# Chunk-local scores with a carried state, and the transfers that put K~ in chunk order, in a gated linear attention kernel with an MLP

## The chip, the cores and the metric

The kernel runs on one core of one Trainium2 chip. The metric is the device time of one execution in microseconds (us). Most executions of one kernel agree within about 1%; where I give a time it is the median of the runs, with the lowest and the highest where that matters. A single run of the kernel before, 1021.7 us at a granted clock of 0.766 beside six at 837 to 840 us, was slow and is left out. (The granted clock is the share of its full clock that TensorE was given.)

## The reference, cut to what matters

```
# attention: B=4, H=8, S=768, D=48, float32
mag = sqrt(a_re^2 + a_im^2);  a = (a_re + i a_im) * min(mag, 0.999) / (mag + 1e-6)
for t in range(S):
    S_t = a[t] (per row d, complex) * S_{t-1} + k[t] v[t]^T      # D x D, complex
    y[t] = Re( q[t] S_t )
# then an MLP on 3072 rows of 384
x = y as (B*S, H*D)
out = relu(x @ w_in)^2 @ w_out          # 384 -> 2048 -> 384
```

The kernel doesn't step through time. With P(t) the running product of the decays, Q~ = q P and K~ = k / P (rows of 2 x 48 = 96 for real and imaginary parts), and y[t] is the sum over s <= t of (Q~[t] . K~[s]) v[s]. That sum can be cut: scores within a chunk of 128 steps, and everything older through a 96 x 48 state, the sum of K~[s] v[s]^T over the earlier chunks.

## The kernel before

(Excerpts of code, here and below, are shortened; `...` marks cuts.)

A *unit* is 384 steps of one batch entry: the first or the second ("late") half of a sequence. There are 8 units of 4 head pairs. VectorE computes decays, running products and K~, Q~ of one unit; TensorE does the pair work of another and the MLP (`hidden`, `project`) of a third, so three units are in flight.

The inputs lie with three steps in a row: step s = 3p + c is at partition p, place c. That makes the loads long and serves the scan. Scores and output need chunk order instead: step s of chunk j at partition s - 128j. For Q~ and K~ this happens on the way through the transposes (`turn`), whose copies to SBUF interleave the three places. The state product contracts over time, so any order will do if K~ and V have the same: the kernel loads V a second time in row order (`vn`) for it.

```
LOADS: step s = 3p + c at partition p        # C = 128 partitions, W = 3, R = 96, HH = 4
def score(u, i, h):                          # per head: 384 + 128 (+ 256 for two heads at once)
    nc.tensor.matmul(sa[:, 0:3], lhsT=kt[:, 0:C], rhs=qt)          # chunk 0 against all 384
    nc.tensor.matmul(sa[:, 3], lhsT=kt[:, 2*C:3*C], rhs=qt[:, 2*C:3*C])
    dve.tensor_tensor(out=A[:, h, 0:4:3], in0=sa[:, 0:4:3], in1=mask2, op=ALU.mult)
    act.copy(out=A[:, h, 1:3], in_=sa[:, 1:3])                     # unmasked blocks
    ...                                                            # chunk 1 against 256
def keep(u, i):                              # first half only: state at its end
    ... nc.tensor.matmul(ps[:, h], lhsT=K~[:, hh, c], rhs=u["vn"][:, hh, c],
                         start=(c == 0), stop=(c == W - 1))
def mix(u, i):                               # output of a head pair, transposed
    ...
    act.copy(out=yt[0:64 + D], in_=ypair[0:64 + D])
    # to the rows of xT where the MLP wants them: pieces of 48, 32 or 16 rows
    nc.sync.dma_start(out=u["xT"][r % C:r % C + n, r // C], in_=yt[p:p + n])
def hidden(u, f):                            # waits for all of the unit's xT
    ... nc.tensor.matmul(ps, lhsT=w1[:, f, m], rhs=u["xT"][:, m])
```

The loads of the attention inputs, the xT transfers and the stores of the result are issued from SyncE's queue, in order (SPq in the views below); the loads of the weights are on GpSimd's.

Of the kernel before, what the change touches and what calls it, by code (L numbers as in the profile page):

```python
# [9 lines left out]
F32 = mybir.dt.float32  # L10
# [5 lines left out]
ALU = mybir.AluOpType  # L16
# [465 lines left out]
def fast_path(ctx, tc, q, k, v, a_re, a_im, moe_w_in, moe_w_out, out, flag):  # L482
# [54 lines left out]
    mask2 = mask.unsqueeze(1).to_broadcast([C, 2, C])  # L537
# [28 lines left out]
    def convert(i):  # L566
# [20 lines left out]
        if i >= NF:  # L587
            after(first, mark["second"])
        elif i >= EARLY:
            after(first, mark["scanned"])  # L590
# [5 lines left out]
    EARLY = 4  # L596
# [18 lines left out]
    def load(u):  # L615
# [21 lines left out]
        if u["half"] < NHALF - 1:  # L637
            u["vn"] = nat.tile([C, H, W, D], F32, name="vn", tag="vn")
            nc.sync.dma_start(out=u["vn"].rearrange("p h c d -> p h (c d)"),
                              in_=src(v).rearrange(LOADS, c=W))  # L640
# [128 lines left out]
    def product(u, dst, x, y):  # L769
# [16 lines left out]
        return dve.tensor_tensor(out=dst[:, 1], in0=f[0][:, 1], in1=f[1][:, 0], op=ALU.add)  # L786

    def scan(u):
# [16 lines left out]
        for m in range(NM):  # L805
            done = product(u, v4[:, :, m, 1:32], v4[:, :, m, 1:32],
                           inc[:, :, m, 0:31].unsqueeze(3).to_broadcast([C, 2, 31, 4]))
        mark.setdefault("scanned", done)
# [14 lines left out]
    def apply(u, z):  # L823
# [15 lines left out]
        t = pr.tile([C, 2, HH, W, 2, D], F32, name="QK", tag="QK")  # L839
        u.setdefault("QK", {})[z] = t  # L840
        for j in range(2):
            for r in range(2):
                done = dve.tensor_tensor(out=t[:, j, :, :, r], in0=qk[:, j], in1=a[:, r],  # L843
                                         op=ALU.mult)
        if u["n"] == 1:
            mark["second"] = done


    def turn(u, i, c):
# [3 lines left out]
        src = u["QK"][2 * i // HH]  # L853
        ps = trp.tile([R, 4, C], F32, name="tq", tag="tr")
        for j in range(2):
            for h in range(2):
                nc.tensor.transpose(  # L857
                    ps[:, 2 * j + h],
                    src[:, j, (2 * i + h) % HH, c].rearrange("p r d -> p (r d)"), ident)
        act.copy(out=u["T"][i].rearrange("r z (p c) -> r c z p", c=W)[:, c], in_=ps)  # L860

    def score(u, i, h):

        T = u["T"][i]
        if h == 0:
            u.setdefault("A", {})[i] = pr.tile([C, 2, 6, C], F32, name="A", tag="A")
        A = u["A"][i]
        if h < 2:
            qt, kt = T[:, h], T[:, 2 + h]
            sa = scp.tile([C, 4, C], F32, name="sa", tag="sc")  # L870
            nc.tensor.matmul(sa[:, 0:3].rearrange("p n t -> p (n t)"), lhsT=kt[:, 0:C],  # L871
                             rhs=qt, start=True, stop=True)
            nc.tensor.matmul(sa[:, 3], lhsT=kt[:, 2 * C:3 * C], rhs=qt[:, 2 * C:3 * C],  # L873
                             start=True, stop=True)
            dve.tensor_tensor(out=A[:, h, 0:4:3], in0=sa[:, 0:4:3], in1=mask2, op=ALU.mult)  # L875
            act.copy(out=A[:, h, 1:3], in_=sa[:, 1:3])  # L876
            return
        sb = scp.tile([C, 2, 2, C], F32, name="sb", tag="sc")
        for h in range(2):
            qt, kt = T[:, h], T[:, 2 + h]  # L880
            nc.tensor.matmul(sb[:, h].rearrange("p n t -> p (n t)"), lhsT=kt[:, C:2 * C],  # L881
                             rhs=qt[:, C:3 * C], start=True, stop=True)
        dve.tensor_tensor(out=A[:, :, 4], in0=sb[:, :, 0], in1=mask2, op=ALU.mult)  # L883
        act.copy(out=A[:, :, 5], in_=sb[:, :, 1])  # L884
# [3 lines left out]
    def keep(u, i):  # L888

        if u["half"] == NHALF - 1:  # L890
            return
        if i == 0:
            state[u["b"]] = wk.tile([R, H, D], F32, name="S", tag="S", bufs=2)
        ps = trp.tile([R, 2, D], F32, name="kv", tag="tr")
        for h in range(2):
            for c in range(W):
# [197 lines left out]
```

## Time and profile before

| | before |
|---|---|
| median of 3 runs | 840.0 us (837.4 to 845.8) |
| span of the profiled run | 839.8 us |
| TensorE busy / idle / after its last instruction | 748.4 / 83.6 / 7.8 us |
| granted TensorE clock, mean | 0.983 |
| first hidden product of units 0, 2, 3, 7 at | 91.9, 309.3, 402.0, 769.7 us |

Busy, idle and tail add up to the span. The last row gives a clock for the stages: from unit 3 to unit 7 a unit takes (769.7 - 402.0) / 4 = 91.9 us.

The prediction below shows the views. In them PE is TensorE, PEld its loading of weights, DVE VectorE, ACT ScalarE, POOL GpSimd, and SPq the transfers issued from SyncE's queue; L945 is a line of the kernel, and `h<-xT,w` names the tile written and those read.

### The profile page before, as it was taken

The page shows a single profiled execution, that of the slowest core. Times are in us where ns is not written, and L with a number is a line of the kernel's source. Part 1 is how long each engine was busy: PE and PEld are TensorE (multiplying, and loading weights), DVE is VectorE, ACT ScalarE, POOL GpSimd, SP SyncE. Part 2 cuts the span into 40 slices and gives each one's busy share as a digit, 9 for nine tenths or more (in the row PEclk, how much of TensorE's full clock was granted, in tenths as well). Part 3 has the DMA queues.
Part 4 walks back from the last instruction along what each step waited for, and adds up shares of the span by engine and source line. Part 5 has one row for each costly group of instructions (what it writes and reads, how often), then busy time and mean ns, then how long its engine had stood idle before and what let it go on. Part 6 is the DMA issues. An engine that isn't in the chain of part 4 may idle for free.

```text
span 839.8 us, 9088 instructions
## 1 busy us (share of the span) xinstructions
PE 748.4 (89%) x3090; PEld 453.8 (54%) x3090; DVE 507.8 (60%) x1284; ACT 436.2 (52%) x865; POOL 43.6 (5%) x75
## 2 busy tenths in 40 slices
PE   0129995999899889999999999999999989999996
PEld 0016553555566556666566656666666646555553
DVE  5997888889989666078642868097825866300000
ACT  5616883765597159611894259623982235422510
POOL 4101000200000000000000000000000143000000
PEclk9999998999999999999999999999999999999998
DMA  9625301740120150002400150004200278200000
GB/s 284 178 64 166 78 0 29 242 127 26 36 87 8 45 162 6 7 17 55 119 8 8 51 161 1 11 14 124 50 9 17 81 232 269 67 16 27 0 10 23
DMA packets 76920, 61.24 MB, mean 73 GB/s; under 512 B 28736, under 2 KB 71744, under 8 KB 76864
## 3 DMA queue, kind: packets, MB, share of 16 engines
q1 hardware_dynamic: 70720, 35.40, 15.2%
q0 software_dynamic: 6144, 25.17, 9.1%
q8 instruction: 26, 0.43, 0.2%
q14 instruction: 30, 0.25, 0.1%
HBM read 51.12 MB, written 4.72 MB: 66 GB/s over the span
## 4 chain that ended last, share of the span: by engine, by line
PE 59%; DVE 15%; issue 12%; DMA 7%; ACT 4%; SPq 1%; POOL 0%; POOLq 0%; ACTq 0%
PE h L945 21%; PE o L959 19%; PE ypair L914 4%; PE sa L871 4%; PE tq L857 3%; DVE fa L782 3%; PE sb L881 2%; DMA look<-in_moe_w_out_dram 2%; PE kv L898 2%; DMA look<-in_moe_w_in_dram 2%; DVE fb L834 1%; DVE QK L843 1%; PE sa L873 1%; PE ypair L910 1%; ACT QKT L860 1%
## 5 line engine op out<-in xcount | busy, mean ns | idle before, releaser
L945 PE MATMUL h<-xT,w 128*128 128x384 f32 x768 | 274.5, 497 | 10.5 <-DMA xT<-yt 8.5
L959 PE MATMUL o<-w,g 128*128 128x384 f32 x768 | 263.3, 490 | 0.0
L945 PEld LDWEIGHTS h<-xT,w 128*128 128x128 f32 x768 | 140.3, 194 | 89.7 <-DMA xT<-yt 10.5
L959 PEld LDWEIGHTS o<-w,g 128*128 128x128 f32 x768 | 141.3, 191 | 85.9 <-issue 4.1
L860 ACT COPY QKT<-tq 96x512 f32<-96x512 f32 x96 | 80.2, 851 | 48.5 <-PE tq L857 46.4
L950 ACT ACTIVATE g<-h 128x384 f32<-128x384 f32 x128 | 61.9, 488 | 66.6 <-PE h L945 66.2
L857 PE MATMUL tq<-ident,QK 128*96 128x128 f32 x384 | 62.7, 291 | 14.3 <-DVE QK L843 12.7
L857 PEld LDWEIGHTS tq<-ident,QK 128*96 128x96 f32 x384 | 46.5, 134 | 43.7 <-issue 27.5
L951 ACT ACTIVATE g<-g 128x384 f32<-128x384 f32 x128 | 66.4, 523 | 2.4
L875 DVE TENSOR_TENSOR A<-sa,mask 128x256 f32<-128x256 f32 x64 | 26.4, 419 | 58.1 <-PE sa L873 57.9
L782 DVE TENSOR_TENSOR fa<-e 128x192 f32<-128x192 f32 (+1 forms) x56 | 23.8, 455 | 60.0 <-ACT e L755 59.4
L871 PE MATMUL sa<-QKT 96*128 96x384 f32 x128 | 55.3, 514 | 0.1
L914 PE MATMUL ypair<-A,v 128*48 128x256 f32 (+2 forms) x384 | 50.3, 387 | 1.1 <-ACT A L884 1.0
L876 ACT COPY A<-sa 128x256 f32<-128x256 f32 x64 | 23.3, 370 | 52.1 <-DVE A L875 52.1
L843 DVE TENSOR_TENSOR QK<-qk,a 128x576 f32<-128x576 f32 x64 | 44.4, 748 | 0.0
L753 PE MATMUL tot<-ident,last 128*128 128x128 f32 x72 | 14.1, 298 | 31.5 <-ACT last L715 28.7
L1037 DVE TENSOR_SCALAR flag<-cnt 1x1 int32<-1x1 f32 x1 | 0.1, 147 | 69.1 <-PE cnt L1036 69.1
L914 PEld LDWEIGHTS ypair<-A,v 128*48 128x48 f32 x384 | 22.7, 123 | 33.3 <-issue 23.8
L963 ACT COPY ot<-o 128x384 f32<-128x384 f32 x24 | 11.4, 475 | 56.2 <-PE o L959 56.2
L607 POOL DMA_DIRECT2D look<-in_moe_w_in_dram x16 | 12.3, 770 | 510.0 <-DVE A L875 496.0
L884 ACT COPY A<-sb 128x256 f32<-128x256 f32 x32 | 11.8, 368 | 46.6 <-DVE A L883 46.6
L873 PEld LDWEIGHTS sa<-QKT 96*128 96x128 f32 x128 | 24.8, 195 | 17.7 <-issue 2.2
(104 smaller groups left out, 921.0 us busy)
## 6 DMA issues: line engine op xcount, KB each, us to landing
raw<-in_moe_w_in_dram POOLq DMA_DIRECT2D x16, 384.0 KB, 5.1
raw<-in_moe_w_out_dram POOLq DMA_DIRECT2D x16, 384.0 KB, 5.2
look<-in_moe_w_in_dram POOLq DMA_DIRECT2D x16, 384.0 KB, 4.2
look<-in_moe_w_out_dram POOLq DMA_DIRECT2D x16, 384.0 KB, 4.1
a<-in_a_re_dram SPq DMA_DIRECT2D x16, 288.0 KB, 3.0
a<-in_a_im_dram SPq DMA_DIRECT2D x16, 288.0 KB, 3.7
qk<-in_q_dram SPq DMA_DIRECT2D x16, 288.0 KB, 5.0
qk<-in_k_dram SPq DMA_DIRECT2D x16, 288.0 KB, 5.1
```

The costliest lines, as they stand in the source:

```text
L782: dve.tensor_tensor(out=t, in0=x, in1=y[:, j].unsqueeze(1).to_broadcast(shape), op=ALU.mult)
L843: done = dve.tensor_tensor(out=t[:, j, :, :, r], in0=qk[:, j], in1=a[:, r], op=ALU.mult)
L857: nc.tensor.transpose(ps[:, 2 * j + h], src[:, j, (2 * i + h) % HH, c].rearrange("p r d -> p (r d)"), ident)
L860: act.copy(out=u["T"][i].rearrange("r z (p c) -> r c z p", c=W)[:, c], in_=ps)
L871: nc.tensor.matmul(sa[:, 0:3].rearrange("p n t -> p (n t)"), lhsT=kt[:, 0:C], rhs=qt, start=True, stop=True)
L873: nc.tensor.matmul(sa[:, 3], lhsT=kt[:, 2 * C:3 * C], rhs=qt[:, 2 * C:3 * C], start=True, stop=True)
L875: dve.tensor_tensor(out=A[:, h, 0:4:3], in0=sa[:, 0:4:3], in1=mask2, op=ALU.mult)
L914: nc.tensor.matmul(ypair[64 * h:64 * h + D, j * C:L], lhsT=u["v"][:, j, 2 * i + h], rhs=A[:, h, lo:hi].rearrange("p n t -> p (n t)"), star ...
L945: nc.tensor.matmul(ps, lhsT=w1[:, f, m], rhs=u["xT"][:, m], start=(m == 0), stop=(m == NM - 1))
L950: act.activation(out=t, in_=ps, func=AF.Relu)
L951: act.activation(out=t, in_=t, func=AF.Square)
L959: nc.tensor.matmul(u["o"], lhsT=u["g"][f][:, ts(c, C)], rhs=w2[:, f], start=(f == 0), stop=(f == NF - 1))
```

## The change

The intent: TensorE is the bound from about 310 us on, and chunk-local scores need fewer columns. Scores are computed in the three diagonal 128 x 128 blocks only; the past comes in by a state per chunk, built from one product per chunk and head and added up on VectorE. Those products need K~ and V of *one chunk* on the partitions, so row order will not do any more: K~ is put in chunk order by transfers within SBUF, and the second load of V goes. In addition all conversions of weights are kept behind the last Q~, K~ product of the first (or second) unit.

```
@@ apply: K~ in chunk order
+        kc = u["KC", z] = nat.tile([C, NM, HH, R], F32, name="KC", tag=f"KC{z}")
+        for j in range(NM - u["half"]):          # chunks: 3, in a late half 2
+            for c in range(W):                   # the three places of a row
+                lo = -(-(j * C - c) // W)
+                hi = -(-((j + 1) * C - c) // W)
+                first = W * lo + c - j * C
+                nc.sync.dma_start(out=kc[first:first + W * (hi - lo - 1) + 1:W, j],
+                                  in_=out_k[lo:hi, c])
@@ score
+        for j in range(NM):
+            nc.tensor.matmul(sa[:, j], lhsT=T[:, 2 + h, ts(j, C)], rhs=T[:, h, ts(j, C)], ...)
+        dve.tensor_tensor(out=u["A"][i][:, h], in0=sa, in1=mask3, op=ALU.mult)
@@ keep
+        for j in range(n):
+            for h in range(2):
+                nc.tensor.matmul(ps[:, j, h], lhsT=u["KC", hh // HH][:, j, hh % HH],
+                                 rhs=u["v"][:, j, hh], start=True, stop=True)
+        ... # first chunk of a sequence: act.copy, then dve.tensor_tensor(add) onto the state
@@ mix: per chunk, A[j] with v[j], and (if there is a past) the state with Q~ of the chunk
@@ load
-            u["vn"] = ...                        # second load of V
@@ convert
-        if i >= NF: after(first, mark["second"])
-        elif i >= EARLY: after(first, mark["scanned"])
+        after(first, mark["QK", i // NF])
```

128 steps at three a row are 42 or 43 rows: for each chunk and half of the heads there are three transfers, of 43, 43 and 42 rows of 1.5 KB, to every third partition. In all there are 120: 18 in a first-half unit and 12 in a late one.

More of the change, by code (lines that the diff above doesn't have):

```diff
@@ L536, in fast_path @@
                        fill=0.0, base=0, channel_multiplier=-1)
-    mask2 = mask.unsqueeze(1).to_broadcast([C, 2, C])
+    mask3 = mask.unsqueeze(1).to_broadcast([C, NM, C])
     sums = const.tile([C, NU, 7], F32, name="sums")
@@ L586, in convert @@
                                   op0=ALU.bitwise_and, op1=ALU.logical_shift_left)
-        if i >= NF:
-            after(first, mark["second"])
-        elif i >= EARLY:
-            after(first, mark["scanned"])
+        after(first, mark["QK", i // NF])
         dve.scalar_tensor_tensor(out=bits, in0=hi, scalar=0xC0000000, in1=bits,
@@ L594, in convert @@
         dve.tensor_tensor(out=bits, in0=bits, in1=more, op=ALU.add)
-    EARLY = 4
     SPARE = ("fa0", "fa1", "fb0", "fb1")
@@ L636, in load @@
                               in_=src(v).rearrange("h (j s) d -> s j h d", s=C)[:, j])
-        if u["half"] < NHALF - 1:
-            u["vn"] = nat.tile([C, H, W, D], F32, name="vn", tag="vn")
-            nc.sync.dma_start(out=u["vn"].rearrange("p h c d -> p h (c d)"),
-                              in_=src(v).rearrange(LOADS, c=W))
     def flat(t):
@@ L785, in product @@
         dve.tensor_tensor(out=dst[:, 0], in0=f[0][:, 0], in1=f[1][:, 1], op=ALU.subtract)
-        return dve.tensor_tensor(out=dst[:, 1], in0=f[0][:, 1], in1=f[1][:, 0], op=ALU.add)
+        dve.tensor_tensor(out=dst[:, 1], in0=f[0][:, 1], in1=f[1][:, 0], op=ALU.add)
     def scan(u):
@@ L805, in scan @@
         for m in range(NM):
-            done = product(u, v4[:, :, m, 1:32], v4[:, :, m, 1:32],
-                           inc[:, :, m, 0:31].unsqueeze(3).to_broadcast([C, 2, 31, 4]))
-        mark.setdefault("scanned", done)
+            product(u, v4[:, :, m, 1:32], v4[:, :, m, 1:32],
+                    inc[:, :, m, 0:31].unsqueeze(3).to_broadcast([C, 2, 31, 4]))
         if u["half"] < NHALF - 1:
@@ L838, in apply @@
                           op=ALU.add)
-        t = pr.tile([C, 2, HH, W, 2, D], F32, name="QK", tag="QK")
-        u.setdefault("QK", {})[z] = t
-        for j in range(2):
-            for r in range(2):
-                done = dve.tensor_tensor(out=t[:, j, :, :, r], in0=qk[:, j], in1=a[:, r],
-                                         op=ALU.mult)
-        if u["n"] == 1:
-            mark["second"] = done
+        t = pr.tile([C, 2 * HH * W * R], F32, name="QK", tag="QK")
+        half = HH * W * R
+        out_q = u["Q", z] = t[:, 0:half].rearrange("p (h c e) -> p h c e", h=HH, c=W)
+        out_k = t[:, half:2 * half].rearrange("p (c h e) -> p c h e", h=HH, c=W)
+        u["K", z] = out_k
+        for j, o in ((1, out_k.rearrange("p c h e -> p h c e")), (0, out_q)):
+            for r in range(2):
+                done = dve.tensor_tensor(out=o[:, :, :, r * D:(r + 1) * D], in0=qk[:, j],
+                                         in1=a[:, r], op=ALU.mult)
+        mark["QK", u["n"]] = done
+        kc = u["KC", z] = nat.tile([C, NM, HH, R], F32, name="KC", tag=f"KC{z}")
[6 more added lines that the diff above has]
+                                  in_=out_k[lo:hi, c])
     def turn(u, i, c):
@@ L852, in turn @@
             u.setdefault("T", {})[i] = pr.tile([R, 4, L], F32, name="QKT", tag="QKT")
-        src = u["QK"][2 * i // HH]
+        z = 2 * i // HH
         ps = trp.tile([R, 4, C], F32, name="tq", tag="tr")
@@ L856, in turn @@
             for h in range(2):
-                nc.tensor.transpose(
-                    ps[:, 2 * j + h],
-                    src[:, j, (2 * i + h) % HH, c].rearrange("p r d -> p (r d)"), ident)
+                hh = (2 * i + h) % HH
+                src = u["K", z][:, c, hh] if j else u["Q", z][:, hh, c]
+                nc.tensor.transpose(ps[:, 2 * j + h], src, ident)
         act.copy(out=u["T"][i].rearrange("r z (p c) -> r c z p", c=W)[:, c], in_=ps)
@@ L865, in score @@
         if h == 0:
-            u.setdefault("A", {})[i] = pr.tile([C, 2, 6, C], F32, name="A", tag="A")
-        A = u["A"][i]
-        if h < 2:
-            qt, kt = T[:, h], T[:, 2 + h]
-            sa = scp.tile([C, 4, C], F32, name="sa", tag="sc")
-            nc.tensor.matmul(sa[:, 0:3].rearrange("p n t -> p (n t)"), lhsT=kt[:, 0:C],
-                             rhs=qt, start=True, stop=True)
-            nc.tensor.matmul(sa[:, 3], lhsT=kt[:, 2 * C:3 * C], rhs=qt[:, 2 * C:3 * C],
-                             start=True, stop=True)
-            dve.tensor_tensor(out=A[:, h, 0:4:3], in0=sa[:, 0:4:3], in1=mask2, op=ALU.mult)
-            act.copy(out=A[:, h, 1:3], in_=sa[:, 1:3])
-            return
@@ L878, in score @@
-        sb = scp.tile([C, 2, 2, C], F32, name="sb", tag="sc")
-        for h in range(2):
-            qt, kt = T[:, h], T[:, 2 + h]
-            nc.tensor.matmul(sb[:, h].rearrange("p n t -> p (n t)"), lhsT=kt[:, C:2 * C],
-                             rhs=qt[:, C:3 * C], start=True, stop=True)
-        dve.tensor_tensor(out=A[:, :, 4], in0=sb[:, :, 0], in1=mask2, op=ALU.mult)
-        act.copy(out=A[:, :, 5], in_=sb[:, :, 1])
+            u.setdefault("A", {})[i] = pr.tile([C, 2, NM, C], F32, name="A", tag="A")
@@ L886, in fast_path @@
+        sa = scp.tile([C, NM, C], F32, name="sa", tag="sc")
+        for j in range(NM):
+            nc.tensor.matmul(sa[:, j], lhsT=T[:, 2 + h, ts(j, C)], rhs=T[:, h, ts(j, C)],
+                             start=True, stop=True)
+        dve.tensor_tensor(out=u["A"][i][:, h], in0=sa, in1=mask3, op=ALU.mult)
     state = {}
     def keep(u, i):
-        if u["half"] == NHALF - 1:
-            return
-        if i == 0:
+        late = u["half"] > 0
+        n = NM - u["half"]
+        if i == 0 and not late:
@@ L893, in keep @@
             state[u["b"]] = wk.tile([R, H, D], F32, name="S", tag="S", bufs=2)
-        ps = trp.tile([R, 2, D], F32, name="kv", tag="tr")
-        for h in range(2):
-            for c in range(W):
+        total_s = state[u["b"]][:, 2 * i:2 * i + 2]
+        ps = trp.tile([R, NM, 2, D], F32, name="kv", tag="tr")
+        for j in range(n):
+            for h in range(2):
                 hh = 2 * i + h
-                nc.tensor.matmul(
-                    ps[:, h],
-                    lhsT=u["QK"][2 * i // HH][:, 1, hh % HH, c].rearrange("p r d -> p (r d)"),
-                    rhs=u["vn"][:, hh, c], start=(c == 0), stop=(c == W - 1))
@@ L902, in keep @@
-        act.copy(out=state[u["b"]][:, 2 * i:2 * i + 2], in_=ps)
+                nc.tensor.matmul(ps[:, j, h], lhsT=u["KC", hh // HH][:, j, hh % HH],
+                                 rhs=u["v"][:, j, hh], start=True, stop=True)
+        st = pr.tile([R, 2, 2, D], F32, name="St", tag="St")
+        u.setdefault("S", {})[i] = [total_s if late else None, st[:, 0], st[:, 1]]
+        outs = [st[:, 0], st[:, 1], total_s]
+        before = total_s if late else None
+        for j in range(n):
+            if before is None:
+                act.copy(out=outs[j], in_=ps[:, j])
+            else:
+                dve.tensor_tensor(out=outs[j], in0=ps[:, j], in1=before, op=ALU.add)
+            before = outs[j]
@@ L904, in mix @@
     def mix(u, i):
         T, A = u["T"][i], u["A"][i]
-        late = u["half"] > 0
-        if late:
+        for j in range(NM):
+            S_j = u["S"][i][j]
             for h in range(2):
-                nc.tensor.matmul(ypair[64 * h:64 * h + D], lhsT=state[u["b"]][:, 2 * i + h],
-                                 rhs=T[:, h], start=True, stop=False)
-        for j, lo, hi in ((0, 0, 3), (1, 4, 6), (2, 3, 4)):
+                nc.tensor.matmul(ypair[64 * h:64 * h + D, ts(j, C)],
+                                 lhsT=u["v"][:, j, 2 * i + h], rhs=A[:, h, j],
+                                 start=True, stop=S_j is None)
@@ L913, in mix @@
             for h in range(2):
-                nc.tensor.matmul(ypair[64 * h:64 * h + D, j * C:L],
-                                 lhsT=u["v"][:, j, 2 * i + h],
-                                 rhs=A[:, h, lo:hi].rearrange("p n t -> p (n t)"),
-                                 start=(j == 0 and not late), stop=(j == 2))
+                if S_j is not None:
+                    nc.tensor.matmul(ypair[64 * h:64 * h + D, ts(j, C)], lhsT=S_j[:, h],
+                                     rhs=T[:, h, ts(j, C)], start=False, stop=True)
@@ L936, in pair_work @@
                 w.append([lambda i=i: mix(u, i - 1)])
-            w += [[lambda i=i, h=h: score(u, i, h)] for h in range(3)]
+            w += [[lambda i=i, h=h: score(u, i, h)] for h in range(2)]
         w += [[], [lambda: mix(u, NP - 1)]]
```

## The prediction

> **What bounds the kernel now.** I read the page's busy shares and slices first, to see which engine is full and when.
>
> ```profile
> PE 748.4 (89%) x3090; PEld 453.8 (54%) x3090; DVE 507.8 (60%) x1284; ACT 436.2 (52%) x865; POOL 43.6 (5%) x75
> ...
> PE   0129995999899889999999999999999989999996
> ...
> DVE  5997888889989666078642868097825866300000
> ```
>
> A slice is 21 us. TensorE is full from slice 15 (about 310 us) to the end; before that VectorE is as full as TensorE or fuller. So there are two regimes. The windows (busy us of PE, its weight loads, DVE, ACT, POOL) put numbers to them.
>
> ```profile
> 40.00:60.00 20.00, 3.42 (x12) 2.05 (x13) 18.60 (x69) 2.81 (x6) 2.14 (x3) 1.00 0.27 86
> ...
> 240.00:280.00 40.00, 37.66 (x174) 24.03 (x171) 36.39 (x106) 29.76 (x64) 0.00 (x0) 0.98 0.08 23
> ...
> 320.00:360.00 40.00, 40.00 (x169) 24.30 (x168) 10.99 (x23) 29.84 (x59) 0.00 (x0) 1.00 0.02 5
> ```
>
> From 0 to about 300 us, three chains of normalisation, scan and products run on VectorE (first unit's products end at 67.8, second's at 150.4, fourth's at 297). From 310 on TensorE alone is the bound. Busy time overlaps there, so I take what an instruction costs from the distance between starts in the timeline of PE (start, length, ..., count).
>
> ```profile
> 653.66 0.60 PE L857 MATMUL tq<-ident,QK 128*96 128x128 f32 x4
> 654.09 1.14 PE L898 MATMUL kv<-vn,QK 128*96 128x48 f32 x12
> 655.07 0.88 PE L959 MATMUL o<-w,g 128*128 128x384 f32 x2
> ...
> 658.14 1.50 PE L914 MATMUL ypair<-A,v 128*48 128x384 f32 x12
> 659.58 0.55 PE L819 MATMUL bk<-ident,e 128*128 128x128 f32 x3
> 659.96 2.75 PE L959 MATMUL o<-w,g 128*128 128x384 f32 x8
> 662.54 0.81 PE L871 MATMUL sa<-QKT 96*128 96x384 f32 x2
> 663.19 0.38 PE L873 MATMUL sa<-QKT 96*128 96x128 f32 x2
> 663.41 1.78 PE L959 MATMUL o<-w,g 128*128 128x384 f32 x5
> ```
>
> One matmul of the source is two records. Two of 384 columns take 0.65 us (662.54 to 663.19), two of 128 take 0.22, so 0.108 us per 128-column record; twelve kv records 0.98 (654.09 to 655.07, 0.082 each); twelve ypair records 1.44 (658.14 to 659.58).
>
> At the changes of unit the chain of waits shows what TensorE lacks for 2 to 3 us: xT, the transfer of the last head pair.
>
> ```profile
> 299.70 0.50 SPq L624 DMA_DIRECT2D qk<-in_q_dram  x1
> ...
> 302.45 1.60 SPq L624 DMA_DIRECT2D qk<-in_k_dram  x1
> ...
> 310.01 1.15 SPq L927 DMA_DIRECT2D xT<-yt  x2
> ```
>
> In this timeline of the transfer queue, xT stands behind eight input loads that waited for VectorE's products; each issue takes about 0.5 us.
>
> [...]384 columns take 0.65 us, 1.68 ns per column[...]; transposes (one record) take half. [...]ypair streams 2 heads x 768 columns, 2.6 us at 1.68 ns, in 1.44. [...]For 256 elements [...]the trace has 419 for the mask. [...]the trace has 1.9 us to landing for the 24 KB and the 48 KB transfers of xT alike.
>
> **The change, part by part.** There are 32 head pairs (8 units of 4), 16 in a first half of a sequence and 16 in a second ("late") half.
>
> Scores. Before, per head 384+128+256 columns, 0.65+0.22+0.43 = 1.30 us, 2.60 a pair. After, six products of 128 columns, 12 records x 0.109 = 1.31. **-1.3 us per pair** on TensorE.
>
> Output. Before 1.44, plus 0.7 late for the state (the L910 row: 13.6 us busy in 64 records that overlap in twos; four start-to-start take 0.68 to 0.78). After, 128-column records, two heads at once: 0.054 each, 20 of them in a first half, 24 late, plus 0.15 for the ends: 1.23 and 1.45. **-0.2 and -0.7**.
>
> State. First half: six products as before, 12 records, 0. Late: none before, four now, 8 x 0.085 = **+0.7**.
>
> Net on TensorE: -1.5 per first-half pair, -1.3 per late pair, -45 us in all. Only part lies where TensorE is the bound: the pairs of units 3 to 7 run after 310 us, 12 late and 8 first: 12 x 1.3 + 8 x 1.5 = **-27.6 us**. Units 0 to 2 carry 17 us, in the regime shared with VectorE.
>
> ScalarE loses the copies of unmasked scores, 64 x 0.370 + 32 x 0.368 = -35 us; the state copies stay at 16 x 0.237. Off the path after 310; a small help before it.
>
> VectorE: masks were 26.4 + 13.4 = 39.8 us, become 64 of 384 elements, [...]The 64 additions of 96 elements are new, [...]VectorE is 40% idle after 310, so nothing there[...]. The products into QK (64 of 748 ns) keep their size and only change their strides.
>
> Transfers: vn goes (4 of 576 KB). 18 transfers for K~ per first-half unit, 12 per late one, 120 in all, of 43 rows x 1.5 KB, at about 0.5 us of issue: 9 or 6 us of the queue per unit, some 2 us to landing. K~ is computed before Q~, so they start about 1.4 us earlier than the products end. I looked at the order of the transfer queue in both: from unit 3 on, the K~ transfers now stand before the last xT and the big input loads after it. That exchanges eight loads (2.3 MB) for 12 to 18 small ones ahead of xT, and ScalarE's copy to yt no longer stands behind an instruction that waits for those loads. I give **-3 us** over the boundaries, which show idle TensorE of 2.2, 1.7, 1.7 and 3.4 us now.
>
> Conversion. Before 67.8 us VectorE does five conversions' worth (four whole, one in pieces), 0.27+0.47+0.47 = 1.21 us each from starts: 6 us, some of it in gaps. The first unit's products come about 5 us earlier, but all 16 conversions (19.4 us) now fall into the first unit's pair work, which took 25.5 us with 11 of them and 7.7 us of idle VectorE. [...]So only 3 us of the 5 survive. Second and third units: TensorE -5 and -6 us, [...]both near full; I give -4 together. **-7 us before 310.**
>
> Sum: -27.6 - 3 - 7 = -38 us: 840 - 38 = **802 us**. The tail from 770 (hidden and projection of the last unit, 62 us) does not change.
>
> **The rivals.** (a) K~ transfers hold the queue. VectorE's last K~ product of a unit is followed by 6 to 9 issues, 3 to 4.5 us, and only then xT; if yt is ready before them, TensorE waits up to 4 us more at each of 6 boundaries: +24, about 826. For it: 0.5 us per issue. Against it: the eight loads it replaces cost the same issue time and more bytes. (b) The additions tie the PSUM buffer of kv to VectorE's in-order stream; transposes share those two buffers and would wait behind chain instructions. Then part of the 27.6 comes back as idle TensorE: about 815. For it: VectorE's chain now and then stands idle waiting for ScalarE. Against it: the mask already couples them so, and score buffers now come free without a second copy. (c) The first 310 us gain nothing, as VectorE gets more work: about 809. (d) TensorE's bubbles shrink too: from 160 us on, start-to-start times exceed the nominal by some 39 us, with half-clock stretches after idle gaps; fewer stalls could give 10 us more: 792.
>
> **Range and chances.** 802 as the sum; (b) and (c) together lead to about 818, (d) to 790. Range 788 to 818. Faster by over 2% is below 823: that is 17 us, under two thirds of the 27.6 alone, so (b) or (c) would still be faster; (a) in full would miss it. Faster 0.92, within 2% 0.07, slower 0.01.
>
> **What would show it.** Score records: 384 of 128 columns with a start-to-start of 0.11 us; the ypair group of a pair 1.2 to 1.5 us; kv 320 records. Phase lengths after 310: about 88 us per unit for 93. ACT's busy time about 400, DVE's about 520. First unit's products end near 62.5 and its conversions near 90. If (a): PE waits of several us on xT with K~ issues before them in the queue. If (b): PE waits on VectorE's additions before transposes. If the ypair records take 0.1 us each, the heads no longer overlap and the output costs 1 us more per pair. The prediction fails most likely through the ordering of the engines' streams, which the sums do not see.

The sum came to -38 us, that is 802. My estimates of what a mask and an addition would cost VectorE: the 520 us of VectorE and the 90 us at which conversions would end rested on them, and of the -7 us before 310 the -3 of the first unit; the other -4 are my estimate for the second and third units.

## More of the kernel before

One group of the page is needed here as well, the hidden products: how many, their busy time, the mean of one, and, behind the bar, TensorE's idle time just ahead of them with what ended it.

```profile
L945 PE MATMUL h<-xT,w 128*128 128x384 f32 x768 | 274.5, 497 | 10.5 <-DMA xT<-yt 8.5
```

TensorE lost 8.5 us in all to waits for xT, the last transfer between attention and MLP.

## The result, and the profile after

The changed kernel took **984.45 us** (983.02 to 985.81, 4 runs), the kernel before 838.68 us (4 runs): a ratio of **1.172**, with a 95% interval of 1.165 to 1.180. It is slower by 17% and right in its result.

| profiled run | before | after |
|---|---|---|
| span, us | 839.8 | 981.1 |
| TensorE busy / idle / tail, us | 748.4 / 83.6 / 7.8 | 743.2 / 230.8 / 7.1 |
| TensorE instructions | 3090 | 3474 |
| granted clock | 0.983 | 0.892 |
| us per unit, units 3 to 7 | 91.9 | 109.2 |

The page after: busy times, then the slices of TensorE, VectorE and the granted clock (one digit is a fortieth of the span).

```profile
PE 743.2 (76%) x3474; PEld 483.8 (49%) x3474; DVE 520.5 (53%) x1316; ACT 404.3 (41%) x769; POOL 44.4 (5%) x75
...
PE   0235685469976996899649993999569970999997
...
DVE  6864569647982694549217670859026861540000
...
PEclk9999797579987897899859996999779995999999
```

VectorE's 520 and ScalarE's 404 us are what was predicted. TensorE's row, which was nearly all nines from slice 15, now has a hole in every unit, down to 0 near the end, and the granted clock falls at the holes (0.66 from 480 to 520 us, where TensorE is busy for 18.9 of 40 us; 1.00 in the 40 us before, where it is busy for 39.9). The 141 us of longer span are 147 us of more idle time. Busy time fell by 5 us only: the products stream fewer columns (in more instructions), but part of them ran at a lower clock.

Which waits? Two groups of the page:

```profile
L941 PE MATMUL h<-xT,w 128*128 128x384 f32 x768 | 284.3, 514 | 82.1 <-DMA xT<-yt 80.8
...
L888 PE MATMUL kv<-v,KC 128*96 128x48 f32 x320 | 41.4, 280 | 64.9 <-DMA KC<-QK 42.3
```

The waits for xT have gone from 8.5 us to 80.8, and the state products wait 42.3 us for K~ in chunk order (KC). Now the transfer queue at one change of unit (start, length, engine, line, transfer, count):

```profile
469.37 26.56 SPq L847 DMA_DIRECT2D KC<-QK  x18
496.04 2.92 SPq L923 DMA_DIRECT2D xT<-yt  x2
499.64 0.43 SPq L620 DMA_DIRECT2D a<-in_a_re_dram  x1
```

And TensorE over the same time (in brackets: idle time before, and what ended it):

```profile
483.51 0.51 PE L888 MATMUL kv<-v,KC 128*96 128x48 f32 x4 [2.87 <-DMA KC<-QK]
489.12 0.85 PE L888 MATMUL kv<-v,KC 128*96 128x48 f32 x4 [5.11 <-issue]
...
506.65 5.94 PE L941 MATMUL h<-xT,w 128*128 128x384 f32 x9 [13.13 <-DMA xT<-yt]
```

The 18 issues, for which I had allowed 9 us, hold the queue for 26.6. xT stands behind them, its own landing comes after that, and TensorE is idle for 13 us. The queue is only part of it: both xT transfers are issued by 499.0 us, and still the products start at 506.65. In the trace's completion records the first of them has 15 of its 16 completions by 499.9 us and the last at 506.3, 0.2 us after that of the last 43-row transfer (506.1): as I read it, one sixteenth of xT waits for an engine that still works on K~. At the other changes of unit the idle time before the hidden products is 8.1, 15.4, 13.0 and, in the last, 28.0 us. So the queue is held, as in my rival (a), but for far longer than by its arithmetic. Why does a transfer of 64.5 KB take so long? The view of transfers in the middle of that stretch (40 slices of 0.65 us) says it:

```profile
GB/s 0 12 17 61 28 64 109 33 24 26 102 28 26 26 24 26 24 26 24 24 26 24 24 24 26 24 24 113 26 26 24 59 80 26 24 24 113 28 24 24
...
KC<-QK SPq DMA_DIRECT2D x12, 64.5 KB
KC<-QK SPq DMA_DIRECT2D x6, 63.0 KB
```

There is a floor of 24 to 26 GB/s for microseconds on end, with short peaks. In the transfer records the rows of a 43-row transfer follow one another every 61 ns, 1536 bytes each: 25 GB/s, and 43 x 61 ns = 2.6 us for one transfer. The six 42-row transfers are the peaks, most of whose rows are done in about 0.25 us each. The completion records fit (packets of 4 bytes, in the view those under 512 B): 90 of them in 470 to 496 us, where 12 transfers on one engine and 6 on fourteen write 12 + 6 x 14 = 96 when all have landed.

I had not counted completions before. In this stretch each 43-row transfer has one data completion, each 42-row one fourteen (both have one more record, some 0.4 us after the end of the issue, which I leave out) and each of the two 48-row transfers of xT sixteen; in the kernel before, every transfer of the program has sixteen, the 128-row ones as well as the 48, 32 and 16 rows of xT. I read their number as that of the engines which took part; the records name none. The data completions of the twelve 43-row transfers come one by one from 474.60 to 506.14 us, 2.7 to 3.1 us apart, and of each 42-row transfer's fourteen the last comes 3.4 to 6.2 us after the others, so all twelve seem to have shared one engine. "On one engine" means this here and below. By their rows alone the twelve of a first-half unit are 12 x 43 x 61 ns = 31.5 us, the 8 of a late one 21 us. xT, which I took as the model for "some 2 us to landing", has sixteen completions for each piece.

### The profile page after: what moved, and what is told of

Same layout as the page of the kernel before. It is cut to its first block, busy times and chain, and to the rows that moved or that the text cites. A ratio compares the mean times of both kernels' runs of the same rounds, so it can differ in the third digit from the quotient of the medians. Undisturbed runs are those within 1.5% of the kernel's fastest.

```text
span 981.1 us, 10011 instructions
## 1 busy us (share of the span) xinstructions
PE 743.2 (76%) x3474; PEld 483.8 (49%) x3474; DVE 520.5 (53%) x1316; ACT 404.3 (41%) x769; POOL 44.4 (5%) x75
## 4 chain that ended last, share of the span: by engine, by line
PE 50%; SPq 17%; DVE 14%; DMA 10%; ACT 6%; issue 2%; ACTq 0%; DVEq 0%
PE h L941 19%; PE o L955 18%; SPq L847 11%; DVE fa L774 5%; DMA xT<-yt 5%; DMA a<-in_a_im_dram 3%; PE sa L871 3%; SPq L620 3%; PE ypair L907 3%; PE tq L861 2%; PE kv L888 2%; PE ypair L912 2%; SPq L631 2%; DMA KC<-QK 1%; DVE fb L777 1%
## 5 line engine op out<-in xcount | busy, mean ns | idle before, releaser
L941 PE MATMUL h<-xT,w 128*128 128x384 f32 x768 | 284.3, 514 | 82.1 <-DMA xT<-yt 80.8
L955 PEld LDWEIGHTS o<-w,g 128*128 128x128 f32 x768 | 140.5, 191 | 84.1 <-issue 3.0
L888 PE MATMUL kv<-v,KC 128*96 128x48 f32 x320 | 41.4, 280 | 64.9 <-DMA KC<-QK 42.3
L888 PEld LDWEIGHTS kv<-v,KC 128*96 128x96 f32 x320 | 38.5, 197 | 73.4 <-issue 54.5
L871 PEld LDWEIGHTS sa<-QKT 96*128 96x128 f32 x384 | 59.0, 222 | 11.2 <-issue 3.2
L871 PE MATMUL sa<-QKT 96*128 96x128 f32 x384 | 63.7, 311 | 0.0
L873 DVE TENSOR_TENSOR A<-sa,mask 128x384 f32<-128x384 f32 x64 | 35.1, 552 | 38.3 <-PE sa L871 38.1
L915 ACT COPY yt<-ypair 112x384 f32<-112x384 f32 x32 | 15.3, 478 | 85.6 <-PE ypair L912 85.5
L648 DVE TENSOR_TENSOR fb<-fa 128x576 f32<-128x576 f32 x16 | 11.9, 755 | 71.3 <-ACT fa L645 71.3
L907 PE MATMUL ypair<-A,v 128*48 128x128 f32 x384 | 44.8, 294 | 0.0
L898 DVE TENSOR_TENSOR St<-kv,St 96x96 f32<-96x96 f32 x32 | 8.0, 250 | 65.4 <-ACT St L896 65.2
## 6 DMA issues: line engine op xcount, KB each, us to landing
KC<-QK SPq DMA_DIRECT2D x80, 64.5 KB
```

What stands on the lines that cost most here:

```text
L871: nc.tensor.matmul(sa[:, j], lhsT=T[:, 2 + h, ts(j, C)], rhs=T[:, h, ts(j, C)], start=True, stop=True)
L888: nc.tensor.matmul(ps[:, j, h], lhsT=u["KC", hh // HH][:, j, hh % HH], rhs=u["v"][:, j, hh], start=True, stop=True)
L907: nc.tensor.matmul(ypair[64 * h:64 * h + D, ts(j, C)], lhsT=u["v"][:, j, 2 * i + h], rhs=A[:, h, j], start=True, stop=S_j is None)
L941: nc.tensor.matmul(ps, lhsT=w1[:, f, m], rhs=u["xT"][:, m], start=(m == 0), stop=(m == NM - 1))
L955: nc.tensor.matmul(u["o"], lhsT=u["g"][f][:, ts(c, C)], rhs=w2[:, f], start=(f == 0), stop=(f == NF - 1))
```

## The experiments

I had four theories for the 182 us between the predicted 802 and the measured 984. (A) The transfers of 43 rows run on one engine. (B) The number of issues and their place ahead of xT in SyncE's queue is what costs, whatever the engines do. (C) The computation itself (products, additions, PSUM buffers) is not as cheap as summed. (D) The step of 3 partitions of the destination makes the transfers slow.

| run | what | median us | ratio to before, 95% interval | result |
|---|---|---|---|---|
| e1_split32 | each transfer cut into 32 + 10 or 11 rows | 851.3 | 1.015 [1.013, 1.018] | right |
| e2_pool | K~ transfers on GpSimd's queue | 829.3 | 0.989 [0.986, 0.991] | right |
| e3_xt_act | xT from ScalarE's queue | 966.4 | 1.153 [1.150, 1.156] | right |
| e4_plain | 3 or 2 plain transfers of 128 rows | 806.1 | 0.962 [0.960, 0.964] | wrong |
| e7_rows48 | 48, 48, 32 rows, step 1 | 821.7 | 0.978 [0.974, 0.982] | wrong |
| e8_rows43 | 43, 43, 42 rows, step 1 | 984.3 | 1.172 [1.168, 1.176] | wrong |
| e5_rule_alone | before, with the new conversion rule only | 839.7 | 0.998 [0.994, 1.002] | right |
| e9_masked_v | no K~ transfers: masked copies of V | 829.6 | 0.988 [0.984, 0.992] | right |
| e10_dram_pool | K~ to DRAM and back, GpSimd's queue | 830.3 | 0.991 [0.986, 0.997] | right |
| e11_dram_two_queues | the same, SyncE's queue out, GpSimd's back | 825.0 | 0.981 [0.975, 0.988] | right |
| e13_two_queues | 32-row pieces on SyncE's, the rest on GpSimd's queue | 823.6 | 0.980 [0.975, 0.984] | right |
| e14_dram_xt_act | e11, and xT from ScalarE's queue | 842.0 | 1.004 [1.001, 1.007] | right |

Each had 3 rounds, e5 and e14 five. Edits are to the changed kernel unless said otherwise. By the 2% that counts as a difference here, e4 is faster, the changed kernel, e3 and e8 are slower, e7, e11 and e13 stay unclear, and the others are the same as before. One caution holds for all of them but e7 and e8: with an edit the scheduler also puts the engines' instructions in another order (in e4 and e3 some 2960 to 2990 of TensorE's 3474 stand where they stand in the changed kernel, in e1 2256, in e13 3462). In e7 and e8 the order on TensorE, VectorE and ScalarE is that of the changed kernel throughout.

### Row count against step: e7_rows48 and e8_rows43

These two are the sharpest pair. Both keep the changed kernel's 120 transfers on SyncE's queue, with the same total of rows, and write without a step, to the wrong partitions (the result is wrong; everything else runs as before). They differ in the row counts and where these cut.

```
e7: +  for c, (lo, hi) in enumerate(((0, 48), (48, 96), (96, 128))):
e8: +  for c, (lo, hi) in enumerate(((0, 43), (43, 86), (86, 128))):
    +      nc.sync.dma_start(out=kc[lo:hi, j], in_=out_k[lo:hi, c])
```

> WRONG RESULT ON PURPOSE, to set apart the number of rows from the number of transfers: the nine (six) K~ transfers per half of the heads as in the changed kernel, on the same queue at the same place, but of 48, 48 and 32 rows at the same rows of source and destination, so without reordering. Theory A (43 rows run on one DMA engine): 800 to 830 us. Theory B (the count of issues in the queue): 950 to 990.

> WRONG RESULT ON PURPOSE, the partner of the run with 48 rows: the same transfers of 43, 43 and 42 rows, rows at distance one as there and not at distance three as in the changed kernel. Theory A: as slow as the changed kernel, 970 to 990 us, or a little less. If the distance of three rows in the destination is what is slow (theory D), it is fast: 800 to 830. Theory B: 950 to 990.

Measured: 821.7 and 984.3 us. Row counts of 43, 43, 42 instead of 48, 48, 32 cost 163 us. At 43 rows the step of 3 costs nothing: e8 without it is as slow as the changed kernel (984.5). Theory D falls and A stands. That the pieces of e8 start at partitions 43 and 86, and not at multiples of 16, isn't the cause either: in its completion records near 471 us a 43-row transfer that starts at partition 0 has one data completion, as one that starts at 43, while the 42-row one that starts at 86 has fourteen. TensorE's waits, first in e7 and then in e8 (total, number, longest, in us):

```profile
PE h L937 <- DMA xT<-yt: 8.2, 5, 2.6
```

```profile
PE h L937 <- DMA xT<-yt: 81.2, 7, 28.2
...
PE kv L884 <- DMA KC<-QK: 50.4, 14, 5.4
```

The transfer queue at the change into unit 5, a late unit with twelve K~ transfers, first in e7 and then in e8:

```profile
480.63 7.49 SPq L844 DMA_DIRECT2D KC<-QK  x12
488.22 1.17 SPq L919 DMA_DIRECT2D xT<-yt  x2
```

```profile
581.97 17.53 SPq L844 DMA_DIRECT2D KC<-QK  x12
599.60 1.17 SPq L919 DMA_DIRECT2D xT<-yt  x2
```

The twelve hold the queue for 7.5 us with 48 and 32 rows and for 17.5 with 43 and 42, and over the whole run the 120 issues held it for 70 us and for 190. In e7's view of transfers of that stretch the K~ rows land 2.0 us after their issue, xT beside them in 2.1:

```profile
KC<-QK SPq DMA_DIRECT2D x8, 72.0 KB, 2.0
KC<-QK SPq DMA_DIRECT2D x4, 48.0 KB, 1.9
xT<-yt SPq DMA_DIRECT2D x2, 72.0 KB, 2.1
```

### The computation without the sorting: e4_plain

```
-            for c in range(W): ... nc.sync.dma_start(out=kc[first:...:W, j], in_=out_k[lo:hi, c])
+            nc.sync.dma_start(out=kc[:, j], in_=out_k[:, j])
```

The same bytes in 40 transfers of 128 rows, in the wrong order (a wrong result).

> WRONG RESULT ON PURPOSE: K~ copied without reordering, three (late: two) transfers of all 128 rows per half of the heads in place of nine (six) of 42 or 43; the same consumers, about the same bytes. What the change is worth where its transfers cost little: by the sums of the prediction 795 to 815 us. Theory A and B both say so. Theory C: no better than 950.

Measured: 806.1 us, 4% faster than before. Its page and its K~ transfers:

```profile
PE 706.7 (88%) x3474; PEld 460.0 (57%) x3474; DVE 517.6 (65%) x1316; ACT 404.4 (50%) x769; POOL 44.6 (6%) x75
```

```profile
KC<-QK SPq DMA_DIRECT2D x40, 192.0 KB, 2.3
```

The engines' instructions are those of the changed kernel in kind and number, and three times the bytes land in 2.3 us. TensorE is busy 41.7 us less than before (748.4 - 706.7), where I had summed 45. So theory C falls: the computation is as cheap as predicted. Against this run the changed kernel's span is 179 us longer: 142.6 us of idle TensorE (230.8 - 88.2) and 36.5 us more of busy time for the same 3474 instructions (743.2 - 706.7), at a granted clock of 0.892 instead of 0.969. By the trace's clock records 84.1 us of the busy time ran at half clock, in e4 29.4 us; half of the difference, 27 us, is an estimate of what the clock took of the 36.5.

Between e4 and e7 lie 15.6 us, for 80 more issues at the same bytes. It is at most this much of theory B that holds, since the order of the instructions differs too. In e7 the 120 issues held the queue for 70 us, in e4 the 40 for 22.

### Keeping the row order right: e1_split32, e2_pool, e3_xt_act

e1 cuts each transfer so that the larger piece has 32 rows:

```
+                for at, end in ((lo, lo + 32), (lo + 32, hi)):
+                    to = first + W * (at - lo)
+                    nc.sync.dma_start(out=kc[to:to + W * (end - at - 1) + 1:W, j], in_=out_k[at:end, c])
```

> The changed kernel with each K~ transfer of 42 or 43 rows cut into one of 32 rows and one of the rest (10 or 11); same bytes, twice the issues, right result. Theory A (a transfer of 43 rows runs on one DMA engine: its 43 records follow each other 61 ns apart, 2.6 us, in the trace of the changed kernel, while the 42-row ones run in bursts): the records of a transfer now overlap, a transfer's issue no longer stalls for 2.3 us, and time falls in spite of twice the issues: 36 issues of some 0.55 us per first-half unit leave about 10 us ahead of the last xT, so 860 to 910 us. Theory B (it is the number of issues ahead of xT in the queue, whatever their rows): worse than 984, some 1040. Theory C (the additions on VectorE and the PSUM buffers hold TensorE): no change, 984.

Measured: 851.3 us, right, some 9 us below the range of theory A and far from B's 1040. Twice as many transfers are 133 us faster. But 240 issues at a mean of 0.66 us hold the queue for 157 us of the span, about as long as the 120 slow ones did (165 us); what went away is the time that the data took after the issue (near 420 us, where the 32-row pieces have sixteen completions each, they land 1.8 to 1.9 us after it). The waits of the state products for KC fell from 42.3 us to 4.0, those of the hidden products for xT from 80.8 to 5.9. It is 30 us slower than e7, which has half the issues.

e2 moves the 120 transfers, 43 rows as they are, to GpSimd's queue:

```
-                nc.sync.dma_start(out=kc[first:first + W * (hi - lo - 1) + 1:W, j],
+                nc.gpsimd.dma_start(out=kc[first:first + W * (hi - lo - 1) + 1:W, j],
```

> The changed kernel with the K~ transfers issued from GpSimd's queue in place of SyncE's; nothing else. Theory A: xT and the input loads are no longer behind them; if GpSimd's path spreads the rows over the engines, kv does not wait either, 800 to 830 us; if not, kv waits for K~ at the start of a unit, 850 to 900. Theory B: 800 to 830 either way. Theory C: 984, no change.

Measured: 829.3 us, right. On the page the transfers land in a median of 4.8 us:

```profile
KC<-QK POOLq DMA_DIRECT2D x80, 64.5 KB, 4.8
```

SyncE's queue is clear of them, but at the changes of unit xT now stands behind four or five input loads again, as before the change: the waits for xT are 15.6 us (8.5 before, 6.8 in e4). The trace shows how the rows were shared out: for the 18 transfers issued from 397 to 410 us GpSimd's queue moved 252 packets of 4608 bytes, three rows each, and 12 with the one row left over of the 43-row transfers, so fourteen or fifteen shares per transfer, and many of them overlap. So a 43-row transfer isn't confined to one engine on this queue, which fits theory A.

e3 takes xT out of the queue instead and leaves the slow transfers in it:

```
-                nc.sync.dma_start(out=u["xT"][r % C:r % C + n, r // C], in_=yt[p:p + n])
+                nc.scalar.dma_start(out=u["xT"][r % C:r % C + n, r // C], in_=yt[p:p + n])
```

> The changed kernel with the xT transfers issued from ScalarE's queue; K~ stays slow on SyncE's. Theory A: TensorE's 81 us of waiting for xT falls to under 20, but the 42 us of kv waiting for K~ grow and the input loads still stand behind the K~ transfers: 880 to 930 us. Theory B (place in the queue alone): 810 to 840. Theory C: 984.

Measured: 966.4 us, 18 us better of the 178 that lie between e4 and the changed kernel, and outside every expected range. The waits for xT did fall under 20 us, to 13.3, but those for KC didn't grow (35.1 us, 42.3 before). In its list of waits the time has gone elsewhere (total, number, longest, in us; the changed kernel has 71.3 and 34.4 in all):

```profile
DVE fb L648 <- ACT fa L645: 98.1, 11, 25.9
...
ACT fa L645 <- DMA a<-in_a_im_dram: 89.2, 9, 17.7
```

Now the input loads of the unit after next stand behind the K~ transfers, and ScalarE and VectorE wait for them. So it isn't enough to take xT out; the queue as a whole is too slow, and whatever stands in it comes late.

### The conversion rule: e5_rule_alone

The edit is to the kernel before: the lines of `convert` in the diff above, and the mark behind the last product.

> The kernel before with the rule for the conversions alone (all of the first weight matrix behind the first unit's last product). By the prediction the first unit's products end some 5 us earlier, and most of that is lost again in its pair work: 834 to 842 us, a difference of -3 +-3 us. If the rule costs (conversions late, PE waiting for w1): 845 to 855.

Measured: 839.7 us over 5 rounds, a ratio of 0.998 with an interval that holds 1. The rule by itself is worth nothing that these runs resolve. The first unit's last product ends at 62.8 us instead of 67.9, but unit 2's hidden products start at 313.0 instead of 309.3, and the rest takes its usual time.

### Ways to the same order without few-row transfers: e9_masked_v, e10_dram_pool, e11_dram_two_queues, e13_two_queues

e9 needs no sorted K~ at all. V is loaded in row order as before, GpSimd makes for each chunk a copy with the steps of other chunks set to 0, and the state products contract K~ in row order with these copies side by side.

```
+                nc.tensor.matmul(ps[:, h, 0:n]..., lhsT=u["K", hh // HH][:, c, hh % HH],
+                                 rhs=u["vm", hh // HH][:, hh % HH, c, 0:n]..., start=(c == 0), stop=(c == W - 1))
+            pool.tensor_tensor(out=vm[:, :, :, j], in0=u["vn"][:, ts(z, HH)], in1=by, op=ALU.mult)
```

> Right result, no K~ transfer at all: K~ stays where VectorE writes it (three steps per row), and GpSimd makes, per half of the heads, copies of V in the same layout with the rows outside a chunk set to zero; kv is then six products of 144 (late 96) columns per pair in place of six (four) of 48. Estimate from the spacing of records: 12 x 0.121 = 1.45 us per first-half pair for 0.98, 12 x 0.085 = 1.02 for 0.68 late, 20 pairs after 310 us: +7 us over the run with plain transfers, so 806 + 7 = 813 us; 808 to 825. Theory C (PSUM buffers and additions) would show in none of these.

Measured: 829.6 us, right, above the expected range. From unit 3 on it takes 86.6 us per unit, near e4's 85.3. What is lost is lost earlier: unit 2's hidden products start at 325.3 us, in e4 at 307.1. That is the stage in which VectorE is the bound, and VectorE's busy time is up by 30 us at the same number of instructions (547.7 against 517.6), 14 us of it before these products. Three rows of e4's groups, and the same three instructions in e9 (busy, mean in ns of one):

```profile
L868 DVE TENSOR_TENSOR A<-sa,mask 128x384 f32<-128x384 f32 x64 | 35.0, 549 | 18.7 <-PE sa L866 18.5
L683 DVE TENSOR_TENSOR fa<-a 128x384 f32<-128x384 f32 x64 | 32.9, 552 | 0.3
...
L825 DVE TENSOR_TENSOR fa<-a,xn 128x576 f32<-128x576 f32 x32 | 22.4, 752 | 1.7 <-ACT xn L811 1.6
```

```profile
L692 DVE TENSOR_TENSOR fa<-a 128x384 f32<-128x384 f32 x64 | 35.8, 597 | 0.3
L881 DVE TENSOR_TENSOR A<-sa,mask 128x384 f32<-128x384 f32 x64 | 35.0, 548 | 19.9 <-PE sa L879 19.9
L841 DVE TENSOR_TENSOR fa<-a,xn 128x576 f32<-128x576 f32 x32 | 29.0, 957 | 3.0 <-ACT xn L820 2.9
```

The same multiplication takes 957 ns instead of 752, while the masking, which has one operand in PSUM, is unchanged at 548. The trace puts the longer times where GpSimd works: beside 40 GpSimd multiplications of 1.39 us each, the 70 VectorE instructions that overlap one of them took 30.2 us more than their kinds take in e4, the other 1246 together 0.3 us; two masks among the 70, with their operand in PSUM, took 545 and 547 ns as ever. Instructions with two SBUF inputs aren't the only ones that grew: the first conversion step, a tensor_scalar with one, grew from 351 to 464 ns in the mean. What of the 18 us at unit 2 comes from this is not isolated: e9 also loads V in row order for all units and has three buffers instead of four for the conversions (`wst`).

e10 and e11 send K~ of half the heads to a scratch tensor in DRAM in one transfer of 128 rows and fetch it in chunk order in another.

```
+        nc.gpsimd.dma_start(out=kd.rearrange("(p c) h r -> p c h r", c=W), in_=out_k)     # e11: nc.sync
+        nc.gpsimd.dma_start(out=kc[:, 0:n], in_=kd.rearrange("(j s) h r -> s j h r", s=C)[:, 0:n])
```

> A right result without any transfer of few rows: K~ of half the heads goes to a scratch tensor in DRAM in one transfer of 128 rows (4.6 KB each) and comes back in chunk order in one more, both on GpSimd's queue (32 transfers of all 16 engines in place of 120). If what is lost between 806 us (plain 128-row transfers) and 984 us is the single engine of the 43-row transfers plus the number of issues, then this is 806 to 820 us and correct. Rival: two hops, each with 2 to 5 us to landing, make the state products wait for KC in every unit; at 4 to 8 us per unit that gives it all back: 830 to 860 us, with waits of the kv products for KC in the trace.

> The same with the first hop on SyncE's queue and the second on GpSimd's, so that SyncE's queue holds 2 issues of about 0.6 us per unit and never waits for the first hop to land. If landing on GpSimd's queue (4.8 us where it was seen) is what costs, this is some us faster than the version with both hops there, 804 to 818 us; if it is not, both agree within 3 us.

Measured: 830.3 and 825.0 us, right, above both expected ranges. The rival that I had named, state products waiting for KC, is not it: those waits are 3.2 and 2.7 us in all. A part is once more the waits of the hidden products for xT, 19.7 and 9.7 us (6.8 in e4). With few K~ issues in SyncE's queue the input loads are issued early and stand before xT again; in e10 four of them did, at the change of unit near 490 us.

e13 shares e1's pieces out between two queues:

```
+                    (nc.sync if at == lo else nc.gpsimd).dma_start(out=kc[to:...:W, j], in_=out_k[at:end, c])
```

> A right result with the 32-row pieces on SyncE's queue and the 10- and 11-row pieces on GpSimd's, so each queue has the 6 to 9 issues per half of the heads that the 48-row transfers had (821.7 us). If the number of issues on SyncE's queue is what is left of the loss at 851 us (18 issues in one queue), this is 818 to 826 us. If landing on GpSimd's queue decides instead, it is as slow as all transfers there, 829 us or more.

Measured: 823.6 us, right, within the expected range and near e7 (821.7), which has as many issues in SyncE's queue. This has the lowest median of the versions with a right result: 2.0% below the kernel before, with an interval of 1.6 to 2.5%, so at the edge of what counts as faster here; e11, at 825.0, can't be told from it. Against e1 it is 28 us faster, for the same transfers. It agrees with B as a second term: after the engines, the number of issues in one queue. The order of the instructions, which differs between the two, is the rival that remains.

### A miss: e14_dram_xt_act

e11 with xT issued from ScalarE's queue, as in e3.

> The version with two hops through DRAM on two queues (825.0 us), and in addition xT issued from ScalarE's queue instead of SyncE's. If what is left against 806 us is xT's place behind the input loads and the K~ issues in SyncE's queue (2.0 to 3.4 us of idle TensorE before the hidden products at four changes of unit), those waits go and it is 808 to 818 us. Rival: the rest of the 19 us lies elsewhere (the order of the streams, memory traffic), or ScalarE's in-order stream delays xT as much; then it stays at 821 to 830 us.

Measured: 842.0 us, slower than e11 by 17 us and no faster than before. The waits for xT did not go (13.3 us, up to 4.4 us each). One more transfer in ScalarE's stream moved the order in which the scheduler put the instructions, on TensorE too, so this run doesn't isolate xT's place. What keeps the right versions at 824 where the plain transfers reach 806 is only partly settled: in e11, 3 of the 19 us are longer waits for xT, and the stages before unit 2's hidden products are 6 us longer (313.0 against 307.1). The rest, and how much the order of the instructions does, stays open.

## Why the prediction was wrong

**The step that failed** is the sentence on transfers: "120 in all, of 43 rows x 1.5 KB, at about 0.5 us of issue: 9 or 6 us of the queue per unit, some 2 us to landing". The 2 us came from xT's transfers, of 48, 32 and 16 rows with sixteen completions each. A 43-row transfer has one and, as I read it, runs on one engine, at 61 ns per row, 2.6 us of that engine, and twelve of them in a unit take 31.5 us one after another. The queue's 9 us were 26.6, and even then the last share of xT landed 8.1 us after its issue began at 498.37 (2.2 us in the median before the change), behind K~ rows on that engine. e7 and e8 show it: 163 us by the row counts alone.

**Rival (a)** named the right mechanism and the right sign to look for, "PE waits of several us on xT with K~ issues before them in the queue". Its size, "up to 4 us more at each of 6 boundaries: +24, about 826", used the same 0.5 us. That e7, with 120 issues as well, of 48 and 32 rows, took 821.7 is no confirmation: its waits for xT are 8.2 us in all, as before the change, so it is near 826 by luck. And the boundaries were not the only place: KC itself comes late (42.3 us of waits, which I hadn't listed), the loads come late, and 36.5 us of the 179 between e4 and the changed kernel are longer busy time, some 27 of them by the lower clock.

**The -3 us at the boundaries** turned into the loss. I compared "eight loads (2.3 MB)" with 12 to 18 small transfers and took the bytes for the cost. The eight loads have 128 rows. Nor did they hold xT in the lines shown: the last of them is issued by 304.1 us, and xT at 310.0, just when ScalarE's copy to yt ended (309.98). What held xT there was that copy, which stood in ScalarE's stream behind an instruction that waited 1.4 us for a load. (A slip without effect: the fourth unit's products end at 299.8 us, not 297.)

**The sums of TensorE were right.** They said -45 us in all and -27.6 - 3 after 310; e4 has -41.7 us of busy time and, from unit 2's to unit 7's hidden products, 425.7 us for 460.4, that is -34.7. A unit takes 85.3 us (predicted 88). 802 was near for e4, which took 806, in part by luck: of the 37.7 us that its span is shorter, 2.2 lie before unit 2's hidden products, where I gave 7, and 34.7 after them, where I gave 30.6, and the two misses cancel.

**Before 310 us, rival (c) was right.** I gave -7; e4's unit 2 starts its hidden products at 307.1 for 309.3, so 2 us. The first products did end early (63.3 predicted 62.5), but the conversions ended at 94.1, where 90 was predicted and 93.4 measured before. e5 shows that the rule by itself gains nothing.

**Rival (b)**, the additions that tie PSUM to VectorE, is not seen as a large cost in e4: its state products wait 3.6 us in all, for the copies of the transposes, and no wait of the transposes for an addition is listed. In the changed kernel an addition takes 250 ns, a mask 552 and a product into QK 752 (748 before).

**Rival (d)** was right in direction: 802 has none of it, and e4's second regime came out 4 us better than the sum. From unit 2's to unit 7's hidden products TensorE was idle for 4.2 us in e4 and for 9.8 before, and it spent no time at half clock, before 10.2 us (three stretches of 3.4 us, which begin at 312.9, 408.5 and 684.9 us, each within 1 us of the end of a gap of 2.2, 1.7 and 3.4 us).

The chances were wrong with it: 0.01 for slower came from a list of rivals that all took the duration of a transfer for granted.

## What to carry to other kernels

Before costing a transfer within SBUF, look at its row count, and in a trace at its data completions. On SyncE's queue here 43 rows had one, 42 fourteen, 16, 32, 48 and 128 sixteen; with one, the rows of 1.5 KB followed one another every 61 ns, 2.6 us in all, and e7 and e8 differ by 163 us by the row counts. Other counts have to be measured. The duration that I read from one transfer (2.2 us for 48 rows, 72 KB) did not carry over to another of nearly the same size in the same queue (43 rows, 64.5 KB). And if a queue in order carries such transfers, count what stands behind them: in e3, with xT on another queue, ScalarE waited 89.2 us for input loads behind K~.
